# Loading q and k of the first four head pairs in 1 KB pieces, with strided transposes, a shorter warm-up and a divided last store

## The chip, the cores and the metric

The kernel runs on one core of one Trainium2 chip. What counts is the device time of one execution in microseconds: 769.0 us before, the median of three runs (768.95 to 770.54). Engines are named as the profile names them: PE (TensorE; PEld is its weight load), DVE (VectorE), ACT (ScalarE), POOL (GpSimd), SP (SyncE). A letter q behind an engine's name is its queue of DMA issues.

## The reference, cut to what matters

```
q, k, v: (4, 8, 576, 64) f32
scores = q @ k^T / sqrt(64), blocks of 64; block i sees block j where i >= j
attn = softmax(scores);  a = attn @ v
x = a as (2304, 512)                      # 4 batches x 576 rows, 8 heads x 64
h = x @ w_in (512 x 1024);  solu = h * softmax(h);  x = LayerNorm(solu) * g_ln @ w_out
h = x @ w_in2 (512 x 2048); x = (h * tanh(softplus(h))) @ w_out2      # output f32 (2304, 512)
```

## The kernel before, in words

The 32 heads are worked off in 16 pairs, by `pair(p, xt)`; two heads of 64 fill the 128 rows of PE. For each pair q, k and v are loaded in their natural layout, position by position, into the tiles `qraw`, `kraw` and `vraw` (two buffers each). `turn` (L680) lays q or k on its side: five fp32 transposes with `ident`, each of a tile of 128 positions by 2 x 64 columns, into a slot of two PSUM banks; 9 blocks of 64 positions are used, so the fifth tile is half empty (k's upper half is zeroed once; q is shifted by 64 rows and its first half tile zeroed once). ACT copies the result into the high part in fp32r (`act_hi`, L329: `kh`, `qh`), DVE takes the remainder as the low part (`dve_lo`, L335: `kl`; L693: `ql`). The scores are three products of these parts, 64 rows of PE per head (L714), for the first ten pairs with a small product that adds the mask (L722), whose operands are two 64-column pieces `low` of the first `qh` and `ql` buffers. Head 1's keys stand in the opposite order of blocks, so that the triangles of two heads fill one rectangle.

Then come the maximum on DVE (L750, L778), the exponential on ACT (L734), the division on POOL (L792), transposes of the weights (L809), and the product with v (L830, L837). The results go into the first MoE (L895 to L958; SoLU and LayerNorm) and that into the second (L1159, L1251, L1283), whose last piece is `moe2_end` (adds at L1317 and L1325, store at L1339). Weights are loaded and split all along (L449 to L511).

At the start `warm_up` (L1429) gives PE 20 transposes of `ident` before any data are there. `keep_on` (L702) puts 14 more such transposes at two places: ahead of pair 1's last score products (L763, p == 1), and in pair 6.

All of this is first recorded as operations of a `Plan` with engine, cost, priority (the table `PRIO`), what they read and write, and their PSUM slots; `Plan.order` (L146) is a list scheduler that puts them in order for every engine, and they are then emitted in that order. Loads are issued by SP (pair 0's q by ACT). A head of q or k takes one or two DMAs whose pieces are the 256 bytes of one position's 64 numbers:

```
out=r(), in_=rows[r0:r0 + QT * P, :].rearrange("(j p) d -> p j d", p=P)
```

`load` (L629) does this for q and for head 0 of k, `load_k` (L645) for head 1 of k with its blocks reversed, in two DMAs.

Of the kernel before, what the change touches and what calls it, by code (L numbers as in the profile page):

```python
# [260 lines left out]
def c_dma(kb):  # L261
    return max(0.53, kb / 260.0)
# [10 lines left out]
def c_act(n, sbuf=False, acc=False, ptr=False):  # L273
    return 0.05 + n / 1170.0 + 0.04 * sbuf + 0.18 * acc + 0.09 * ptr
# [11 lines left out]
def kernel(  # L286
# [17 lines left out]
    P = 128  # L304
# [23 lines left out]
    def act_hi(dst, src, mul=1.0):  # L328
        nc.scalar.activation(out=dst, in_=src, func=AF.Copy, scale=mul)  # L329
# [18 lines left out]
    def ps2(s):  # L348
        return banks[s.at // 2]
# [212 lines left out]
    HP = H // 2  # L562
    NRAW = 2
    EARLY = 2
    WARM = 20
    qraw = Rot(at, "qraw", NRAW, (P, QT, 2, D), F32)
    kraw = Rot(at, "kraw", NRAW, (P, QT, 2, D), F32)
    vraw = Rot(at, "vraw", NRAW, (P, QT, 2, D), F32)
    nc.vector.memset(qraw.tiles[0][0:64, 0, 0, :], 0.0)
    for i in range(NRAW):  # L570
        nc.vector.memset(kraw.tiles[i][64:128, QT - 1, 1, :], 0.0)
    kh_r = Rot(at, "kh", 2, (P, S), F32R)
# [4 lines left out]
    pt_r = [Rot(at, f"pt{t}_", NPT[t], (P, 2 * EXT[t]), F32) for t in range(QT)]  # L577
    ptw_r = Rot(at, "ptw", NPTW, (P, 2, 512), F32)
    PEMASK = 10
    low = (qh_r.tiles[0][:, 0:64], ql_r.tiles[0][:, 0:64])  # L580
    for i, (x, val) in enumerate(zip(low, (1.0, NEG))):
        raw = ptw_r.tiles[0][:, i, 0:64]
        nc.vector.memset(raw, 0.0)
# [32 lines left out]
    def R1(t):  # L616
        return P if t else 64

    def pair(p, xt):
        b, h2 = divmod(p, HP)  # L620

        def pri(tag, i):
            base, step = PRIO[tag + ("_a" if p < 2 else "" if p < 8 else "_b")]
            return base + step * i
# [20 lines left out]
        def load_k():  # L645
            blocks = k[b, 2 * h2 + 1].rearrange("(j p) d -> p j d", p=64)
            nc.sync.dma_start(out=kr.t[0:64, :, 1, :], in_=blocks[:, 8::-2, :])
            nc.sync.dma_start(out=kr.t[64:128, 0:4, 1, :], in_=blocks[:, 7::-2, :])

        m, go = load(lambda: kr.t[:, :, 0, :], k, n0 * S, False, nc.sync)  # L650
        add(SP, 0.92, go, w=[kr.key(0)], prio=pri("load_k", p))
        add(SP, 1.06, load_k, w=[kr.key(1)], prio=pri("load_k", p))
        for tag, r, src, off, pad in (("load_q", qr, q, -64, False),):
            for x in range(2):

                m, go = load(lambda r=r, x=x: r.t[:, :, x, :], src, (n0 + x) * S + off, pad, nc.sync if p else nc.scalar)
                if p:
                    add(SP, max(m * 0.53, 0.92), go, w=[r.key(x)], prio=pri(tag, p))
                else:
                    add(ACT, 0.5 * m, go, w=[r.key(x)], prio=-2000 + x, lat=2.8)  # L660
        for x in range(2):
            rows = v[b, 2 * h2 + x]

# [13 lines left out]
        def flat(s, n):  # L677
            return ps2(s).rearrange("p a c -> p (a c)")[:, 0:n]

        def turn(r, s):  # L680
            for j in range(QT):
                nc.tensor.transpose(ps2(s)[:, j // 4, (j % 4) * P:(j % 4 + 1) * P],  # L682
                                    r.t[:, j].rearrange("p a d -> p (a d)"), ident)

        sk_, sq_ = Slot(2), Slot(2)
        kk_, kq_ = ("tk", p), ("tq", p)
# [2 lines left out]
        add(DVE, c_dve(S), lambda: dve_lo(kl.t, flat(sk_, S), kh.t), r=[kk_, kh.key()], w=[kl.key()], rel=[sk_],  # L689
            prio=pri("te", p))  # L690
        add(PE, 0.54, lambda: turn(qr, sq_), r=[qr.key(0), qr.key(1)], w=[kq_, qh.key(), ql.key()], acq=[sq_], prio=pri("tr", p))
        add(ACT, c_act(QT * P), lambda: act_hi(qh.t[:, 64:], flat(sq_, QT * P)[:, 64:], scale), r=[kq_], w=[qh.key()], prio=pri("te", p))
        add(DVE, c_dve(QT * P), lambda: nc.vector.scalar_tensor_tensor(  # L693
            out=ql.t[:, 64:], in0=flat(sq_, QT * P)[:, 64:], scalar=scale, in1=qh.t[:, 64:].bitcast(F32), op0=ALU.mult, op1=ALU.subtract),
            r=[kq_, qh.key()], w=[ql.key()], rel=[sq_], prio=pri("te", p))

        on_pe = p < PEMASK
# [4 lines left out]
        def keep_on(dst, n):  # L702
            for _ in range(n):
                nc.tensor.transpose(dst[:, 0:P], ident, ident)

        def mm(items):

            for i, (a, m) in enumerate(((qh, kh), (ql, kh), (qh, kl))):
                for x, t, c0, c1, dst in items:
                    if p == 6 and t == 4 and x == 1 and c0 == i == 0:  # L710
                        keep_on(ps2(s4[0])[:, 1, :], 14)
                    hs = slice(x * D, (x + 1) * D)
                    o = (S - EXT[t]) * x
                    nc.tensor.matmul(out=dst[:R1(t)], lhsT=a.t[hs, (t + 1) * P - R1(t):(t + 1) * P], rhs=m.t[hs, o + c0:o + c1],  # L714
                                     start=(i == 0), stop=(i == 2))
                if i:
                    continue
                for x, t, c0, c1, dst in items if on_pe else ():
                    hs = slice(x * D, (x + 1) * D)
                    a0 = 0 if x else EXT[t] - 64  # L720
                    if t and c0 <= a0 < c1:
                        nc.tensor.matmul(out=dst[0:64, a0 - c0:a0 - c0 + 64], lhsT=low[0][hs], rhs=low[1][hs],  # L722
                                         start=False, stop=False, skip_group_check=True)
# [34 lines left out]
        for ts in (((3, 0), (0, 448)), ((1, 0), (2, 192))):  # L758
            s = Slot(2)
            sk = ("s", p, ts[0][0])  # L760

            def go(s=s, ts=ts):
                if p == 1 and ts[0][0] == 3:  # L763
                    keep_on(ps2(s)[:, 0, :], 14)
                for t, o in ts:
                    mm([(x, t, 0, EXT[t], ps2(s)[:, x, o:o + EXT[t]]) for x in range(2)])

            add(PE, 0.85, go, mode=1, r=qk,
                w=[sk] + [pts[t].key(x) for t, _ in ts for x in range(2)], acq=[s], prio=pri("sc", p))
# [529 lines left out]
    def moe2_end(cnt, g, i, acc):  # L1299
# [36 lines left out]
        to(o1, 2, 1, 1, 0, [acc[2]])  # L1336
        to(o2, 3, 0, 0, 2, [acc[3]])
        for ob, y in tiles:
            add(SP, c_dma(410), lambda ob=ob, y=y: nc.sync.dma_start(out=out[y * P:(y + 1) * P, :], in_=ob.t),  # L1339
                r=[ob.key(0), ob.key(1)] + alias(ob), w=[("out", y)], prio=pri("store", 0))  # L1340

# [198 lines left out]
```

## Time and profile before

| | |
|---|---|
| median of three runs | 769.0 us |
| profiled execution | 769.02 us |
| its span in the profile | 767.2 us |
| PE busy | 754.6 us, 98% |
| DVE, ACT, POOL busy | 566.5, 443.9, 250.1 us |
| share of PE in the chain that ended last | 89% |
| DMA packets, mean rate | 108840, 154 GB/s |
| packets under 512 bytes | 66016 |

The span is what the profiler saw from the first to the last instruction or transfer; the execution's time has 1.8 us around it. In the tables below a time of one instruction is that of its record. Records of PE overlap, as the end of a matmul is modelled, so the step from the start of one to the start of the next tells what one costs, and its record is longer. "x5" joins five neighbours of one kind, and the time beside it goes from the first's start to the last's end. In square brackets stands how long the engine was idle before, and what released it.

### The profile page before, as it was taken

The numbers are of one execution on the slowest core, as the hardware profiler recorded it, in microseconds if no ns is written. First come the engines' busy times: TensorE is split into PE (matmuls) and PEld (weight loads), VectorE is DVE, ScalarE is ACT, GpSimd is POOL, SyncE is SP. The second block draws the span as 40 slices with busy tenths as digits, with TensorE's granted clock in tenths as the row PEclk, the third lists the DMA queues.
The fourth block names the chain that finished last, engine by engine and source line by source line (L and its number), as shares of the span: only waits on it lengthen the run. The fifth ranks groups of instructions, "written<-read, shape, count | busy, mean of one in ns | idle before, by whom it ended". The sixth has DMA issues, their size and how long they took to land.

```text
span 767.2 us, 14951 instructions
## 1 busy us (share of the span) xinstructions
PE 754.6 (98%) x5604; PEld 688.5 (90%) x5604; DVE 566.5 (74%) x1177; ACT 443.9 (58%) x938; POOL 250.1 (33%) x299
## 2 busy tenths in 40 slices
PE   8899999999999999999999999999999999999997
PEld 7788888788888899999998989989988999999997
DVE  6989889999898998876435797562243588569995
ACT  5998897685657555443427554454454664354560
POOL 2687877784574324563130242110000000000000
PEclk9999999999999999999999999999999999999999
DMA  8764653235344364432375566772276571282203
GB/s 190 185 150 98 163 122 108 85 84 174 110 124 149 107 187 130 158 134 79 115 241 195 199 232 224 284 284 77 96 261 205 183 291 56 97 300 76 92 1 111
DMA packets 108840, 118.14 MB, mean 154 GB/s; under 512 B 66016, under 2 KB 77792, under 8 KB 108768
## 3 DMA queue, kind: packets, MB, share of 16 engines
q1 hardware_dynamic: 107504, 116.88, 48.1%
q8 instruction: 44, 0.72, 0.4%
q10 hardware_dynamic: 1264, 0.31, 0.2%
q14 instruction: 28, 0.23, 0.1%
HBM read 76.27 MB, written 40.89 MB: 153 GB/s over the span
## 4 chain that ended last, share of the span: by engine, by line
PE 89%; DVE 6%; ACT 1%; DMA 1%; POOL 1%; issue 1%; SPq 0%; DVEq 0%; ACTq 0%
PE ps L1159 23%; PE ps L895 13%; PE ps L1283 13%; PE ps L958 12%; PE ps L1251 11%; PE ps L714 5%; PE ps L809 4%; PE ps L830 4%; PE ps L942 2%; DVE nmx L778 1%; PE ps L837 1%; PE ps L682 1%; POOL pt L792 1%; ACT pt L734 1%; DVE kl L335 1%
## 5 line engine op out<-in xcount | busy, mean ns | idle before, releaser
L1159 PE MATMUL ps<-wk,w2ih 128*128 128x384 f32 x576 | 147.0, 336 | 1.1 <-ACT xt L1167 1.1
L1159 PEld LDWEIGHTS ps<-wk,w2ih 128*128 128x128 f32 x576 | 102.4, 188 | 2.8 <-ACT xt L1167 1.3
L895 PE MATMUL ps<-wk 128*128 128x512 f32 x432 | 104.6, 396 | 0.0
L792 POOL TENSOR_SCALAR pt<-pt,sm 128x192 f32<-128x192 f32 (+4 forms) x160 | 91.5, 591 | 32.7 <-DVE sm L728 15.7
L1159 PE MATMUL ps<-wk,w2il 128*128 128x384 f32 x288 | 96.8, 336 | 0.0
L895 PEld LDWEIGHTS ps<-wk 128*128 128x128 f32 x432 | 79.4, 188 | 17.1 <-issue 1.1
L734 ACT ACTIVATE pt<-ps,nmx 128x576 f32<-128x576 f32 (+4 forms) x160 | 81.7, 526 | 20.4 <-DVE nmx L778 11.2
L511 POOL TENSOR_TENSOR wem<-wem 128x512 f32<-128x512 f32 x40 | 56.2, 1407 | 83.1 <-DVE wem L508 67.0
L958 PE MATMUL ps<-lth,woh 128*128 128x256 f32 x288 | 81.6, 283 | 0.0
L958 PE MATMUL ps<-lth,wol 128*128 128x256 f32 x288 | 80.9, 281 | 0.0
L958 PE MATMUL ps<-ltl,woh 128*128 128x256 f32 x288 | 80.8, 280 | 0.0
L1283 PE MATMUL ps<-w2oh,cl 128*128 128x512 f32 x144 | 56.1, 390 | 0.0
L958 PEld LDWEIGHTS ps<-lth,wol 128*128 128x128 f32 x288 | 55.1, 191 | 0.1
L1251 PE MATMUL ps<-w2oh,cl 128*128 128x256 f32 x196 | 55.1, 281 | 0.0
L958 PEld LDWEIGHTS ps<-lth,woh 128*128 128x128 f32 x288 | 54.0, 188 | 0.9 <-issue 0.5
L958 PEld LDWEIGHTS ps<-ltl,woh 128*128 128x128 f32 x288 | 54.1, 188 | 0.3
L1159 PEld LDWEIGHTS ps<-wk,w2il 128*128 128x128 f32 x288 | 54.1, 188 | 0.0
L809 PE MATMUL ps<-ident,pt 128*128 128x128 f32 (+1 forms) x400 | 51.0, 274 | 1.5 <-DVE kl L335 0.6
L809 PEld LDWEIGHTS ps<-ident,pt 128*128 128x128 f32 (+1 forms) x400 | 44.6, 141 | 7.5 <-issue 3.3
L778 DVE TENSOR_REDUCE nmx<-ps 128x2 f32<-128x896 f32 (+1 forms) x64 | 40.9, 682 | 6.1 <-PE ps L714 4.3
L506 ACT ACTIVATE wem<-wem,edges 128x512 int32<-128x512 int32 x40 | 29.0, 728 | 19.8 <-DVE wem L452 19.6
L1171 DVE TENSOR_TENSOR xt<-ps,xt 128x384 f32<-128x384 f32 x26 | 14.4, 553 | 33.0 <-PE ps L1159 16.5
(181 smaller groups left out, 1964.5 us busy)
## 6 DMA issues: line engine op xcount, KB each, us to landing
blk_d<-wk SPq DMA_DIRECT2D x36, 384.0 KB, 2.9
wk<-blk_d SPq DMA_DIRECT2D x36, 384.0 KB, 5.4
wraw<-in_moe_w_in_dram SPq DMA_DIRECT2D x24, 512.0 KB, 4.4
park_d<-wem SPq DMA_DIRECT2D x20, 448.0 KB, 2.6
wraw<-in_moe_w_out_dram SPq DMA_DIRECT2D x16, 512.0 KB, 3.8
wem<-park_d SPq DMA_DIRECT2D x18, 448.0 KB, 4.1
qraw<-in_q_dram SPq DMA_DIRECT2D x30, 160.0 KB, 3.2
x_d<-xo SPq DMA_DIRECT2D x18, 256.0 KB, 2.4
```

The lines of the kernel that those rows point to most:

```text
L511: add(POOL, c_tt(wd), lambda: nc.gpsimd.tensor_tensor(out=mf(), in0=mf(), in1=ex().bitcast(F32), op=ALU.mult), r=[ek], w=[mk], **pt)
L714: nc.tensor.matmul(out=dst[:R1(t)], lhsT=a.t[hs, (t + 1) * P - R1(t):(t + 1) * P], rhs=m.t[hs, o + c0:o + c1], start=(i == 0), stop=(i == 2))
L734: add(ACT, c_act(EXT[t], acc=True), lambda: nc.scalar.activation(out=pp.t[0:R1(t), x * EXT[t]:(x + 1) * EXT[t]] if t < 4 else pp.t[:, x * ...
L778: add(DVE, 2 * c_dve(512), lambda s=s, ts=ts: [nc.vector.tensor_reduce(out=nmx.t[0:R1(t), :, t], in_=ps2(s)[0:R1(t), :, o:o + EXT[t]], axi ...
L792: nc.gpsimd.tensor_scalar(pp, pp, sm.t[0:R1(t), x, t:t + 1], 1.0, op0=ALU.mult, op1=ALU.mult)
L809: nc.tensor.transpose(ps2(s)[:, a, o + P - n:o + P], pts[t].t[0:n, c * P:(c + 1) * P], ident[0:n, 0:n])
L830: nc.tensor.matmul(out=ps(os_[r])[x * D:(x + 1) * D, o:o + n_], lhsT=vr.t[:, j, x, :], rhs=packs[pi].t[:, a, c0:c0 + n_], start=(i in (0, ...
L895: nc.tensor.matmul(out=ps2(hp)[:, hf, :], lhsT=x.t[:, kk, :], rhs=w[:, kk, hf * 512:(hf + 1) * 512], start=bool(first), stop=bool(last))
L958: nc.tensor.matmul(out=ps(s)[:, (c % 2) * 256:(c % 2) * 256 + 256], lhsT=w[:, kk, cs], rhs=x.t[:, kk, :], start=(kk == 0 and i == 0), stop ...
L1159: nc.tensor.matmul(out=ps(s)[:, 0:HT], lhsT=sl_i[j, w][:, c, a, :], rhs=x.t[:, mv], start=(start and c == 0 and i == 0), stop=(c == 1 and ...
L1251: nc.tensor.matmul(out=ps(acc[bi])[:, h * 256:(h + 1) * 256], lhsT=x.t[:, a], rhs=sl_o[j, w][:, b], start=(first and h == 0 and y == 0), s ...
L1283: nc.tensor.matmul(out=ps(acc[t]), lhsT=x.t[:, 2 * t + f], rhs=plain(j, w, f), start=(first and f == 0 and y == 0), stop=(last and f == 1 ...
```

## The change

For pairs 0 to 3 (`WIDE`) q and k are loaded in pieces of four positions, 1 KB each: partition p gets positions 4p to 4p+3 of the head (of q from position 64 on, of k's head 0 from 0 on, of head 1 from 64 on), and the 64 positions that remain of each head come as a small DMA for both heads. The number of DMAs that SP issues for a pair stays (k three in two steps of the plan, q two); pair 0's q has two instead of three on ACT. `turn` follows for these pairs with 9 transposes instead of 5: for head 1 four of 128 columns, of which the upper 64 rows of the result are used and the lower ones written over; for head 0 four of 64 columns; and one of 64 rows for both heads' ends. The first eight write every fourth column of the PSUM bank (head 1 of k with the blocks reversed).

For pairs 4 to 15 the pieces stay at 256 bytes, and the fifth transpose is now one of 64 rows. All pairs have q's last 64 positions in the last place, so the memset of `qraw` is gone, the tiles are read by `q_at`, and the mask's `low` pieces move to columns 576 to 640. The warm-up has 14 transposes. Pair 1's 14 idle ones are left out, pair 6's stay. The last output tile's store is two DMAs of 256 columns each. The order of everything else, and the PSUM banks, are those of before on every engine.

```diff
-    WARM = 20
+    WARM = 14
+    WIDE = 4
...
-    nc.vector.memset(qraw.tiles[0][0:64, 0, 0, :], 0.0)
...
-    low = (qh_r.tiles[0][:, 0:64], ql_r.tiles[0][:, 0:64])
+    low = (qh_r.tiles[0][:, S:], ql_r.tiles[0][:, S:])
...
+    def q_at(t):
+        return slice((t - 1) * P, t * P) if t else slice(512, 576)
...
+        wide = p < WIDE
+
+        def most(r):
+            return r.t.rearrange("p j x d -> p (j x d)")[:, 0:8 * D]
+
+        def q_wide(x):
+            eng = nc.sync if p else nc.scalar
+            heads = q[b, 2 * h2:2 * h2 + 2]
+            if x:
+                eng.dma_start(out=qr.t[0:64, 4], in_=heads[:, 0:64].rearrange("x p d -> p x d"))
+            else:
+                eng.dma_start(out=most(qr).rearrange("p (x c) -> p x c", x=2),
+                              in_=heads[:, 64:].rearrange("x (p j) d -> p x (j d)", j=4))
+
+        def k_wide(x):
+            head = k[b, 2 * h2 + x]
+            rows = head[64:] if x else head[0:512]
+            nc.sync.dma_start(out=most(kr)[:, 4 * D * x:4 * D * (x + 1)], in_=rows.rearrange("(p j) d -> p (j d)", j=4))
+            if x:
+                ends = k.rearrange("b h s d -> (b h s) d")[n0 * S + 512:n0 * S + 640]
+                nc.sync.dma_start(out=kr.t[0:64, 4], in_=ends.rearrange("(x p) d -> p x d", x=2))
...
         def turn(r, s):
-            for j in range(QT):
-                nc.tensor.transpose(ps2(s)[:, j // 4, (j % 4) * P:(j % 4 + 1) * P],
-                                    r.t[:, j].rearrange("p a d -> p (a d)"), ident)
+            if wide:
+                to = ps2(s)[:, 0, :].rearrange("p (a c j) -> p j a c", a=8, j=4)
+                for x in (1, 0):
+                    for j in range(4):
+                        a = 4 * D * x + j * D
+                        o = to[0:D + D * x, j]
+                        nc.tensor.transpose(o[:, ::-1] if x and r is kr else o, most(r)[:, a - D * x:a + D], ident)
+                y, o = r.t[0:64, 4], 0
+            else:
+                a = 0 if r is kr else 1
+                for j in range(4):
+                    nc.tensor.transpose(ps2(s)[:, 0, j * P:(j + 1) * P], r.t[:, j + a].rearrange("p x d -> p (x d)"), ident)
+                o = 64 * a
+                y = r.t[o:o + 64, 0 if a else 4]
+            nc.tensor.transpose(ps2(s)[:, 1, 0:64], y.rearrange("p x d -> p (x d)"), ident[o:o + 64, o:o + 64])
...
-                if p == 1 and ts[0][0] == 3:
-                    keep_on(ps2(s)[:, 0, :], 14)
...
+            if last_group(cnt) and i == 2 and ob is o2:
+                for h in (1, 0):
+                    add(SP, c_dma(205), lambda ob=ob, y=y, h=h: nc.sync.dma_start(
+                        out=out[y * P:(y + 1) * P, h * 256:(h + 1) * 256], in_=half_of(ob, h)),
```

The places in the order that the prediction speaks of follow. In a row stand the line, the operation, the PSUM tile that is written (`ps_63` to `ps_66` are the four two-bank tiles), what it reads, and the size; `qraw_96`, `qraw_97`, `kraw_98` and `kraw_99` are the two buffers of each. Rows of the changed kernel have its own line numbers: L712 and L717 are the transposes of a wide and of a narrow turn, L720 the last one of 64 rows, L751 the scores, L844 the weights' transposes.

PE at the start of the program, before:

```order
L1429 MATMUL ps_63<-ident 128x128 x20
L682 MATMUL ps_63<-ident,qraw_96 128x128 x5
L682 MATMUL ps_64<-ident,kraw_98 128x128 x5
L682 MATMUL ps_65<-ident,kraw_99 128x128 x5
L714 MATMUL ps_66<-kh_105,qh_109 128x288
```

and changed:

```order
L1470 MATMUL ps_63<-ident 128x128 x14
L712 MATMUL ps_63<-ident,qraw_96 128x128 x4
L712 MATMUL ps_63<-ident,qraw_96 64x128 x4
L720 MATMUL ps_63<-ident,qraw_96 128x64
L712 MATMUL ps_64<-ident,kraw_98 128x8x16 x4
L712 MATMUL ps_64<-ident,kraw_98 64x128 x4
L720 MATMUL ps_64<-ident,kraw_98 128x64
L712 MATMUL ps_65<-ident,kraw_99 128x8x16 x4
L712 MATMUL ps_65<-ident,kraw_99 64x128 x4
L720 MATMUL ps_65<-ident,kraw_99 128x64
L751 MATMUL ps_66<-kh_104,qh_108 128x288
```

Six transposes of the warm-up are gone, and the turns of pair 0's q and k and of pair 1's k have 27 instead of 15 ahead of the first scores.

PE ahead of pair 1's scores, before:

```order
L714 MATMUL ps_65<-kl_107,qh_109 128x320 x2
L682 MATMUL ps_66<-ident,qraw_96 128x128 x5
L682 MATMUL ps_63<-ident,qraw_97 128x128 x5
L704 MATMUL ps_63<-ident 128x128 x14
L714 MATMUL ps_63<-kh_106,qh_110 128x448 x2
```

and changed:

```order
L751 MATMUL ps_65<-kl_106,qh_108 128x320 x2
L712 MATMUL ps_66<-ident,qraw_96 128x128 x4
L712 MATMUL ps_66<-ident,qraw_96 64x128 x4
L720 MATMUL ps_66<-ident,qraw_96 128x64
L712 MATMUL ps_63<-ident,qraw_97 128x128 x4
L712 MATMUL ps_63<-ident,qraw_97 64x128 x4
L720 MATMUL ps_63<-ident,qraw_97 128x64
L751 MATMUL ps_63<-kh_105,qh_109 128x448 x2
```

The idle transposes between q's turns and the scores are gone, and the two turns have 18 transposes instead of 10.

PE at the first turns of pair 4, the first narrow ones, before:

```order
L682 MATMUL ps_64<-ident,kraw_98 128x128 x5
L682 MATMUL ps_66<-ident,qraw_96 128x128 x5
L809 MATMUL ps_65<-ident,pt_1_116 128x128
L809 MATMUL ps_65<-ident,pt_1_118 128x128
L809 MATMUL ps_65<-ident,pt_1_120 128x128
```

and changed:

```order
L717 MATMUL ps_64<-ident,kraw_98 128x128 x4
L720 MATMUL ps_64<-ident,kraw_98 128x64
L717 MATMUL ps_66<-ident,qraw_96 128x128 x4
L720 MATMUL ps_66<-ident,qraw_96 128x64
L844 MATMUL ps_65<-ident,pt_1_115 128x128
L844 MATMUL ps_65<-ident,pt_1_117 128x128
L844 MATMUL ps_65<-ident,pt_1_119 128x128
```

Each turn's fifth transpose has become one of 64 columns; what follows stands where it stood.

## Rows read from the trace of the kernel before

**Rows 1.** The page: span, busy time of each engine, chain that ended last by engine.

```profile
span 767.2 us, 14951 instructions
PE 754.6 (98%) x5604; PEld 688.5 (90%) x5604; DVE 566.5 (74%) x1177; ACT 443.9 (58%) x938; POOL 250.1 (33%) x299
PE 89%; DVE 6%; ACT 1%; DMA 1%; POOL 1%; issue 1%; SPq 0%; DVEq 0%; ACTq 0%
```

**Rows 2.** Stretches: length, busy PE PEld DVE ACT POOL, clock, DMA, GB/s.

```profile
25.00:110.00 85.00, 83.63 (x988) 70.86 (x987) 75.24 (x130) 75.43 (x211) 68.80 (x94) 1.00 0.58 141
110.00:195.00 85.00, 84.32 (x710) 70.56 (x709) 79.06 (x163) 62.48 (x151) 58.10 (x77) 1.00 0.41 116
```

**Rows 3.** Timeline and chain, first 9 us: start, duration, what.

```profile
1.34 4.33 PE L1429 MATMUL ps<-ident 128*128 128x128 f32 x20 [1.34 <-POOL ident masks.py:199]
3.95 3.81 DMA kraw<-in_k_dram
5.84 0.74 PE L682 MATMUL ps<-ident,qraw 128*128 128x128 f32 x5 [0.17 <-DMA qraw<-in_q_dram]
7.80 0.77 PE L682 MATMUL ps<-ident,kraw 128*128 128x128 f32 x5 [0.68 <-DMA kraw<-in_k_dram]
8.50 0.53 PE L714 MATMUL ps<-kh,qh 64*128 64x288 f32 x4
```

**Rows 4.** Timeline of PE at two places near 238 and 240 us.

```profile
237.94 0.47 PE L809 MATMUL ps<-ident,pt 128*128 128x128 f32 x2
238.15 0.13 PEld L809 LDWEIGHTS ps<-ident,pt 64*128 64x128 f32 x1 [0.17 <-issue]
238.35 0.44 PE L942 MATMUL ps<-ident,e 128*128 128x128 f32 x2
...
239.93 0.38 PE L942 MATMUL ps<-ident,e 128*128 128x128 f32 x2
240.25 0.44 PE L830 MATMUL ps<-ptw,vraw 128*64 128x256 f32 x2
```

**Rows 5.** Timeline, 11 to 25 us.

```profile
11.63 1.49 PE L682 MATMUL ps<-ident,qraw 128*128 128x128 f32 x10
12.50 1.31 ACT L329 ACTIVATE qh<-ps 128x576 fp32r<-128x576 f32 x2 [0.20 <-PE ps L682]
14.65 1.75 PE L704 MATMUL ps<-ident 128*128 128x128 f32 x14 [1.53 <-DVE ql L693]
17.51 1.28 DVE L778 TENSOR_REDUCE nmx<-ps 128x2 f32<-128x896 f32 x2 [0.76 <-PE ps L714]
18.89 0.63 ACT L734 ACTIVATE pt<-ps,nmx 128x448 f32<-128x448 f32 x1 [0.86 <-DVE sm L728]
21.01 0.77 PE L682 MATMUL ps<-ident,qraw 128*128 128x128 f32 x5 [1.58 <-ACT pt L734]
21.73 0.76 PE L682 MATMUL ps<-ident,kraw 128*128 128x128 f32 x5
22.39 1.06 PE L809 MATMUL ps<-ident,pt 128*128 128x128 f32 x8
23.62 0.77 PE L682 MATMUL ps<-ident,kraw 128*128 128x128 f32 x5 [0.17 <-DVE ql L693]
```

**Rows 6.** Turns from 25 us on: group by form, and two places of the chain.

```profile
L682 PE MATMUL ps<-ident,kraw 128*128 128x128 f32 x60 | 9.1, 282 | 0.2 <-ACT pt L734 0.2
...
108.89 1.24 PE ps L682 x10
...
157.71 1.09 PE ps L682 x10
```

**Rows 7.** The end: timeline, and DMA issues (KB each, us to landing).

```profile
763.40 0.41 DVE L1317 TENSOR_TENSOR xo<-ps,xo 128x256 f32<-128x256 f32 x1
763.93 0.38 SPq L1339 DMA_DIRECT2D out_dram<-xo  x1
...
out_dram<-xo SPq DMA_DIRECT2D x9, 256.0 KB, 2.0
```

More of the change, by code (lines that the diff above doesn't have):

```diff
@@ L648, in load_k @@
             nc.sync.dma_start(out=kr.t[64:128, 0:4, 1, :], in_=blocks[:, 7::-2, :])
-        m, go = load(lambda: kr.t[:, :, 0, :], k, n0 * S, False, nc.sync)
[L651 to L660, printed above, removed]
+        wide = p < WIDE
@@ new lines, in pair @@
+        add(SP, 0.92, (lambda: k_wide(0)) if wide else go, w=[kr.key(0)], prio=pri("load_k", p))
+        add(SP, 1.06, (lambda: k_wide(1)) if wide else load_k, w=[kr.key(1)], prio=pri("load_k", p))
+        for x in range(2):
+            m, go = load(lambda x=x: qr.t[:, :, x, :], q, (n0 + x) * S - 64, False, nc.sync)
+            if wide:
+                go = lambda x=x: q_wide(x)
+            if p:
+                add(SP, max(m * 0.53, 0.92), go, w=[qr.key(x)], prio=pri("load_q", p))
+            else:
+                add(ACT, 0.5 * m, go, w=[qr.key(x)], prio=-2000 + x, lat=2.8)
@@ L680, in turn @@
         def turn(r, s):
-            for j in range(QT):
-                nc.tensor.transpose(ps2(s)[:, j // 4, (j % 4) * P:(j % 4 + 1) * P],
-                                    r.t[:, j].rearrange("p a d -> p (a d)"), ident)
+            if wide:
+                to = ps2(s)[:, 0, :].rearrange("p (a c j) -> p j a c", a=8, j=4)
[5 more added lines that the diff above has]
+                y, o = r.t[0:64, 4], 0
+            else:
+                a = 0 if r is kr else 1
[4 more added lines that the diff above has]
+            nc.tensor.transpose(ps2(s)[:, 1, 0:64], y.rearrange("p x d -> p (x d)"), ident[o:o + 64, o:o + 64])
         sk_, sq_ = Slot(2), Slot(2)
@@ L691, in pair @@
         add(PE, 0.54, lambda: turn(qr, sq_), r=[qr.key(0), qr.key(1)], w=[kq_, qh.key(), ql.key()], acq=[sq_], prio=pri("tr", p))
-        add(ACT, c_act(QT * P), lambda: act_hi(qh.t[:, 64:], flat(sq_, QT * P)[:, 64:], scale), r=[kq_], w=[qh.key()], prio=pri("te", p))
+        add(ACT, c_act(QT * P), lambda: act_hi(qh.t[:, 0:S], flat(sq_, S), scale), r=[kq_], w=[qh.key()], prio=pri("te", p))
         add(DVE, c_dve(QT * P), lambda: nc.vector.scalar_tensor_tensor(
-            out=ql.t[:, 64:], in0=flat(sq_, QT * P)[:, 64:], scalar=scale, in1=qh.t[:, 64:].bitcast(F32), op0=ALU.mult, op1=ALU.subtract),
+            out=ql.t[:, 0:S], in0=flat(sq_, S), scalar=scale, in1=qh.t[:, 0:S].bitcast(F32), op0=ALU.mult, op1=ALU.subtract),
             r=[kq_, qh.key()], w=[ql.key()], rel=[sq_], prio=pri("te", p))
@@ L713, in mm @@
                     o = (S - EXT[t]) * x
-                    nc.tensor.matmul(out=dst[:R1(t)], lhsT=a.t[hs, (t + 1) * P - R1(t):(t + 1) * P], rhs=m.t[hs, o + c0:o + c1],
+                    nc.tensor.matmul(out=dst[:R1(t)], lhsT=a.t[hs, q_at(t)], rhs=m.t[hs, o + c0:o + c1],
                                      start=(i == 0), stop=(i == 2))
@@ L1338, in moe2_end @@
         for ob, y in tiles:
+            if last_group(cnt) and i == 2 and ob is o2:
+                for h in (1, 0):
+                    add(SP, c_dma(205), lambda ob=ob, y=y, h=h: nc.sync.dma_start(
+                        out=out[y * P:(y + 1) * P, h * 256:(h + 1) * 256], in_=half_of(ob, h)),
+                        r=[ob.key(h)] + alias(ob), w=[("out", y, h)], prio=pri("store", 0))
+                continue
             add(SP, c_dma(410), lambda ob=ob, y=y: nc.sync.dma_start(out=out[y * P:(y + 1) * P, :], in_=ob.t),
```

## The prediction

> **What bounds the kernel now.** I read first the page's share of busy time and the chain that ended last [rows 1]: TensorE (PE) is busy for 754.6 us of a span of 767.2, and 89% of the chain lies on PE, 6% on VectorE (DVE), 1% each on ScalarE (ACT) and on DMA. So PE time that is added on the chain is added to the span, nearly one for one, and a faster transfer is worth something only where PE waits for it. Next I read PE's busy time by stretch [rows 2]: of the 170 us from 25 to 195, in which the pairs 4 to 15 are worked off, PE stands idle for 170.00 - 83.63 - 84.32 = 2.05 us. There is hardly a hole in which added PE work could vanish. Then the start [rows 3], the prices of PE's steps [rows 4], the stretch from 11 to 25 us [rows 5], the places of the turns on the chain [rows 6] and the end [rows 7].
>
> The profiled execution took 769.02 us, which is the median of the three runs (769.0), so the sum below can be put on either.
>
> **The price of a step.** A transpose in a run of its like costs what 14 idle ones show: 1.75 us, less some 0.33 that the last one is still recorded after its start, is 13 steps of 0.109 us [rows 5]. A change of the tile's shape costs more. In [rows 4] two transposes begin at 237.94, the first of 128 rows and the second of 64 (the weight load of the second is the row at 238.15), and the next one of 128 rows begins at 238.35: 0.41 us for two steps, 0.20 into the 64-row one and 0.20 out of it. From 239.93 to 240.25 there are two 128-row transposes and then a matmul with a 128x64 stationary: 0.32 - 0.109 = 0.21 for the step to half the columns. So I take 0.20 for every change of shape.
> A turn of five was 5 x 0.109 = 0.545 us. **Narrow turn** (pairs 4 to 15): three steps of 0.109, one into the 64-row transpose, one out of it, 0.73: +0.18 each. **Wide turn** (pairs 0 to 3): 3 x 0.109, 0.20 to half columns, 3 x 0.109, 0.20 to the 64 rows, 0.20 out, 1.25: +0.71 each.
> The Trainium skill ("TensorE: Matmul & The Clock Gate", section "Back-to-back issue gap") gives 64 columns about 60 cycles against 134 for 128, by which the 64-row transpose would be cheaper than the one that it replaces. The rows above have 0.20 there, so the measurement decides; what the rule would make of the time is the first rival.
>
> **A, the start (0.0).** Before, 20 transposes run from 1.34 to 5.67 at 0.213 a step, twice 0.109, so at the lower of the two clock levels (1.2 against 2.4 GHz); q's five begin at 5.84 and end 0.74 us later, 4 x 0.109 and 0.30 for the last one's record, so they have the step of the upper level, and the rise came ahead of them; I put it at 5.4 us. The third turn waits for the k of pair 1, issued at 3.95 and landed at 7.76, and the scores begin at 8.50 [rows 3]. After, 14 transposes end at 1.34 + 14 x 0.213 = 4.3 us. If the 1 KB pieces have landed by then, three wide turns take 3.78 us, and half of the time up to 5.4 is lost to the lower level: 4.4 + 0.5 + 3.8 = 8.7, less the last step out, which disappears since the scores have 64 rows as well: 8.5. What the transfers give, the 12 added transposes take. Bounds: no added price, -0.7; transfers no faster than before, third turn from 7.80, scores at 9.1, +0.6. Both ends stay. The moved `low` columns, the dropped memset and one DMA issue less on ACT cost nothing: nobody waits for them there, since PE's first wait is for q [rows 3].
>
> **B, 11.6 to 18.9 us (+0.45).** Two turns for q begin at 11.63; ACT's two copies (12.50, 1.31 us together) follow, then DVE's low halves, and the idle transposes, which had to wait for these (1.53 us), begin at 14.65 [rows 5]. Two wide turns finish 1.42 us later, the second copy and low half move by about 1.25, and the scores, with 1.75 us of idle transposes gone, begin at 16.4 (14.65 + 1.75) + 1.25 - 1.75 = 15.9. That gain isn't kept: DVE, 1.25 late, has only the 0.76 us that it waited ahead of pair 1's maximum (17.51) to give back, so the maximum and ACT's exponentials behind it (18.89, with 0.86 of wait) come 0.45 to 0.5 later. Bounds: -0.76 (both waits closed by earlier scores) and +1.25.
>
> **C, 21.0 to 24.4 us (+1.75).** Three wide turns stand here, at 21.01, 21.73 and 23.62: 3 x 0.71 = 2.13. Eight transposes of 0.109 from 22.39 end at 23.26, the third turn began at 23.62: 0.36 us of slack, so 2.13 - 0.36 = 1.77 [rows 5]. Bounds: 0.7 (the third turn alone) and 2.1.
>
> **D, pairs 4 to 15 (+1.5).** 60 transposes of k [rows 6] are 12 turns, and there are 12 of q: 24 x 0.18 = 4.4 us of PE. On the chain stand 6 of the 24, of which [rows 6] has the first two and the last two: 6 x 0.18 = 1.1. The others lie where the chain goes through DVE or ACT, and there PE can take up at most its visible idle time of 2.05 us [rows 2], which leaves 2.4. Between 1.1 and 2.4 I take 1.5, nearer to the chain's count, because waits shorter than a matmul's modelled tail don't show as idle. Bounds 0 (as if a 64-row step cost no more) and 4.4.
>
> **E, the end (-0.3).** The last add ends at 763.81, the store of xo is issued at 763.93 and the span ends at 767.2 [rows 7]. Half of that store now goes ahead of the other tile's, and half as many bytes are left behind the last add. A 256 KB store takes 2.0 us from issue to landing [rows 7]; most of that can't be bytes, as the transfer has the tile before it to follow. Bounds -0.6 and 0.
>
> **Sum:** 0.0 + 0.45 + 1.75 + 1.5 - 0.3 = +3.4; 769.0 + 3.4 = **772.4 us**.
>
> **The rivals.**
> *Switches are free* (not slower). If a narrow instruction costs its columns and the load of its weights is pulled ahead, a wide turn is 8 x 0.109 + 0.055 = 0.93 (+0.38), and the last of a narrow one saves 0.055. Start -0.7, B 0 (DVE's 0.76 covers it), C 3 x 0.38 - 0.36 = +0.8, D 24 x -0.055 = -1.3, of which as in D a third counts, -0.5, end -0.3: -0.7, 768.3. It decides below about 0.13 us a switch. Against it stand the steps of [rows 4]; for it, that those are seen at a few places and with other neighbours. Chance 0.13.
> *The transfers set everything up to 24 us* (faster). If PE's extra transposes are as good as free and data are there by 6 us, the scores start 1.5 earlier (the third turn from 6.3 instead of 7.80), pair 1's follow without the idle transposes (-0.76), C is 0, D and the end give -0.8 as above: 766.0. For it: the waits for DMA and DVE in [rows 3, 5]; against: 98% busy PE. Chance 0.09.
> *The clock rises later.* With a shorter warm-up, and gaps if data are late, the rise at 5.4 may come behind the turns: at most 3.4 us more (the 3.8 us of turns at half speed), 775.8. Against it: before, nothing but transposes had run when the step fell from 0.213 to 0.109 [rows 3]. Or PE, idle longer ahead of pair 1's scores without the 14 transposes, falls back to the lower level there. Together 0.06. The Trainium skill ("TensorE: Matmul & The Clock Gate", section "Part 4: PE-mode transpose") says that transposes don't count as busy for the clock; the trace disagrees, by the step that halves after 20 of them.
> *Writes with a stride cost.* 64 wide transposes write every fourth column. No row of before has such a write; at 0.03 us each, 1.9 us in all, 774.3. Chance 0.07.
> *The change doesn't do what it says*: 1 KB pieces land no earlier, A is +0.6, 773.0. Chance 0.05.
>
> **How the numbers follow.** Forecast 0.60, mostly within 770.6 and 774.2. A measurement of this kernel tells apart about 0.2%, 1.5 us. Faster by more: the second rival and a third of the first, 0.13. Within: the rest of the first and the low tail of the forecast (D and C near their lower ends), 0.18. Slower: 0.69. The range 767.6 to 775.0 leaves out the transfers' rival (0.09), most of the clock's (0.06), and the ends of the stride's and the first one's (0.05).
>
> **What would show it.** PE's rows of the turns: 24 with a fifth transpose that begins 0.20 after the fourth, and its follower 0.20 after that; 8 that take 1.25 us from first to next. The scores of pair 0 at 8.5, of pair 1 at 15.9, DVE's first maximum of pair 1 at 18.0, PE at +2.2 where the third wide turn ends, +3.7 at 195 us and from there on constant. If the steps at the 64-row transposes are 0.06 to 0.11, the sum falls and the first rival holds; if scores start below 7.5, the second; if the turns at the start have steps of 0.2 throughout, the clock's.

## The result, and the profile of the changed kernel

The changed kernel takes 773.02 us (median of six runs, 772.47 to 776.23), before 769.05 in the same comparison: a ratio of 1.0052, with an interval of 1.0034 to 1.0070, or +4.0 us. Forecast were +3.4 us, 772.4, slower with a chance of 0.69.

The profiled execution is the longest of the six, 776.23 us, with a span of 774.4, and it is 3.2 us above the median for reasons that can be read, a late rise of the clock and a fall. The lines of the page that answer to [rows 1]:

```profile
span 774.4 us, 14974 instructions
PE 765.8 (99%) x5616; PEld 696.1 (90%) x5616; DVE 566.8 (73%) x1176; ACT 445.5 (58%) x938; POOL 250.0 (32%) x299
PE 95%; DVE 3%; ACT 1%; issue 0%; POOL 0%; DVEq 0%; POOLq 0%; ACTq 0%
```

PE has 11.2 us more than before [rows 1] and its weight loads 7.6; DVE, ACT and POOL are within 1.6 us of what they had. Of the chain that ended last 95% lie on PE, before 89%. By stretch (columns as in [rows 2]; the number behind POOL's is the granted clock):

```profile
6.00:25.00 19.00, 16.79 (x140) 13.66 (x139) 13.53 (x32) 12.94 (x39) 6.66 (x12) 0.81 0.60 164
25.00:110.00 85.00, 84.97 (x939) 72.15 (x939) 73.09 (x125) 73.61 (x204) 64.02 (x89) 0.98 0.58 143
110.00:195.00 85.00, 84.62 (x722) 68.67 (x720) 76.60 (x156) 64.21 (x158) 58.13 (x74) 1.00 0.38 103
...
14.00:16.00 2.00, 1.06 (x9) 0.72 (x7) 0.89 (x2) 1.49 (x3) 0.00 (x0) 1.00 0.01 3
16.00:18.00 2.00, 1.41 (x18) 1.26 (x20) 1.83 (x7) 2.00 (x11) 0.47 (x1) 0.92 0.70 199
18.00:20.00 2.00, 2.00 (x20) 1.80 (x20) 2.00 (x7) 2.00 (x8) 2.00 (x4) 0.50 0.87 211
...
26.00:28.00 2.00, 2.00 (x11) 1.71 (x10) 0.74 (x1) 1.42 (x6) 1.05 (x3) 0.52 0.61 139
28.00:30.00 2.00, 2.00 (x19) 1.74 (x18) 1.32 (x3) 1.68 (x6) 0.00 (x0) 1.00 0.57 130
```

The hole of 2.05 us from 25 to 195 is down to 0.41. And the clock is at the lower level, 0.50, from about 17.7 to 27.9 us: it falls behind the place where the 14 idle transposes stood (PE busy for 1.06 of 2 us from 14 to 16). Of the three wide turns that follow, the first two (22.08 and 24.28) run at half speed, the third doesn't:

```profile
24.28 1.97 PE L712 MATMUL ps<-ident,kraw 128*128 128x128 f32 x8
...
28.09 1.04 PE L712 MATMUL ps<-ident,kraw 128*128 128x128 f32 x8
```

This run has a mean clock of 0.993, the other five have 0.997 to 0.999, so less of it. The mean leaves the start out: the profiles give the first 6 us as 1.00, though the warm-up's steps there are 0.213 us, those of the lower level [rows 3]. A late rise lowers no mean.

PE's timeline shows the prices (start, duration, what):

```profile
1.34 3.25 PE L1470 MATMUL ps<-ident 128*128 128x128 f32 x14 [1.34 <-POOL ident masks.py:199]
4.39 1.91 PE L712 MATMUL ps<-ident,qraw 128*128 128x128 f32 x8
6.52 1.52 PE L712 MATMUL ps<-ident,kraw 128*128 128x128 f32 x8
9.21 0.58 PE L751 MATMUL ps<-kh,qh 64*128 64x288 f32 x4
...
12.53 1.09 PE L712 MATMUL ps<-ident,qraw 128*128 128x128 f32 x8 [0.19 <-ACT pt L771]
13.56 0.27 PE L720 MATMUL ps<-ident,qraw 64*128 64x64 f32 x1
13.76 1.09 PE L712 MATMUL ps<-ident,qraw 128*128 128x128 f32 x8
...
16.59 0.47 PE L751 MATMUL ps<-kh,qh 64*128 64x448 f32 x2 [1.53 <-DVE ql L730]
18.61 1.26 DVE L813 TENSOR_REDUCE nmx<-ps 128x2 f32<-128x896 f32 x2
...
37.40 0.66 PE L717 MATMUL ps<-ident,kraw 128*128 128x128 f32 x4
37.98 0.27 PE L720 MATMUL ps<-ident,kraw 64*128 64x64 f32 x1
38.19 0.66 PE L717 MATMUL ps<-ident,qraw 128*128 128x128 f32 x4
38.77 0.27 PE L720 MATMUL ps<-ident,qraw 64*128 64x64 f32 x1
38.98 0.66 PE L844 MATMUL ps<-ident,pt 128*128 128x128 f32 x4
```

A wide turn takes 13.76 - 12.53 = 1.23 us (forecast 1.25), a narrow one 38.19 - 37.40 = 0.79 (forecast 0.73). The starts of the single transposes tell why. A narrow turn's steps are 164, 109, 109, 203 and, out of the 64-row one, 203 ns: the step out and the step in are the forecast's 0.20, but the first transpose after a change of rows also takes 164 instead of 109 (in the rows: three steps of a narrow turn are 0.66 less the 0.27 of one record, 0.39, where 3 x 0.109 is 0.33). A wide turn's are 164, 109 x 6, 203 and 204: there is nothing at the place where the stationary operand (the one that is loaded ahead, here the data) goes from 128 to 64 columns, and the writes to every fourth column cost nothing. The 1.23 us came out right because two errors in it cancel.

The way from one kernel to the other can be followed at two places, the first 24 products with v that are on the chain, and the run of 213 matmuls near its end. Of before:

```profile
28.53 2.31 PE ps L830 x24
736.81 25.10 PE ps L1251 x213
```

and of the changed kernel:

```profile
33.25 2.31 PE ps L865 x24
744.36 25.10 PE ps L1286 x213
```

Up to the first place +4.72 us, from there to the second another 7.55 - 4.72 = 2.83, and from the second to the end -0.3 (774.4 - 744.36 = 30.04 against 767.2 - 736.81 = 30.39, with spans rounded to 0.1).

### The profile page after: what moved, and what is told of

It is laid out like the page before. It is cut to its first block, busy times and chain, and to the rows that moved or that the text cites. A ratio compares the mean times of both kernels' runs of the same rounds, so it can differ in the third digit from the quotient of the medians.

```text
span 774.4 us, 14974 instructions
## 1 busy us (share of the span) xinstructions
PE 765.8 (99%) x5616; PEld 696.1 (90%) x5616; DVE 566.8 (73%) x1176; ACT 445.5 (58%) x938; POOL 250.0 (32%) x299
## 4 chain that ended last, share of the span: by engine, by line
PE 95%; DVE 3%; ACT 1%; issue 0%; POOL 0%; DVEq 0%; POOLq 0%; ACTq 0%
PE ps L1194 23%; PE ps L930 13%; PE ps L1318 13%; PE ps L993 12%; PE ps L1286 11%; PE ps L844 6%; PE ps L751 5%; PE ps L865 4%; PE ps L977 2%; PE ps L717 2%; PE ps L712 1%; PE ps L872 1%; PE ps L720 1%; DVE nmx L813 1%; ACT pt L771 1%; PE ps L1470 0%
## 5 line engine op out<-in xcount | busy, mean ns | idle before, releaser
L844 PE MATMUL ps<-ident,pt 128*128 128x128 f32 (+1 forms) x400 | 50.6, 277 | 0.0
L844 PEld LDWEIGHTS ps<-ident,pt 128*128 128x128 f32 (+1 forms) x400 | 44.8, 142 | 4.7 <-issue 2.5
```

What stands on the lines that cost most here:

```text
L844: nc.tensor.transpose(ps2(s)[:, a, o + P - n:o + P], pts[t].t[0:n, c * P:(c + 1) * P], ident[0:n, 0:n])
```

## The experiments

Five rounds each. Most expectations set two theories against each other: by that of the steps the whole loss is PE's dearer turns, by that of the clock a part of it is the fall to the lower level. "At full clock" means the runs whose mean clock is 0.999 or 1.000. The kernel before, run beside each experiment, has 768.4 to 769.4 there in all but three of its runs (771.4, 771.6, and one of 1907 that is in no ratio), and 769.2 to 773.0 in those with 0.997 or 0.998. A mean of 0.998 stands for some 1.5 us of lost clock in 770, so the longest of these probably have another cause too; no trace shows it.

**1. The idle transposes back in the changed kernel** (e1_idle_back).

```diff
             def go(s=s, ts=ts):
+                if p == 1 and ts[0][0] == 3:
+                    keep_on(ps2(s)[:, 0, :], 14)
```

> The changed kernel with pair 1's 14 idle transposes put back, nothing else. Theory of the steps (the whole loss is PE's dearer steps in the turns): the idle transposes cost 0 to 0.5 us, 773.0 to 773.5, and the turns at 22 us stay as long as in the changed kernel in a run at full clock. Theory of the clock (without them PE falls to the lower clock level at about 18 us, as the profiled run of the changed kernel shows from 17.8 to 28): granted clock 1.00 in every stretch behind 6 us, and 1.5 to 2.5 us faster than the changed kernel, 770.5 to 771.5.

Measured: 775.17 us, ratio 1.0072 (1.0055 to 1.0088). The runs fall into two groups: 773.06 and 773.53 with a clock of 1.000, and 774.8 to 775.7 with 0.998. The profiled one is of the first group and has a clock of 1.00 in every stretch. Both theories miss. The idle transposes do hold the clock there in this run, but four of six have a lower mean; where the clock fell in these no trace shows, and they are 2.2 us longer, more than 0.998 accounts for. Even at full clock the kernel is slower than the changed one at its best (772.47 with 0.999). So by these few runs leaving them out is worth 0.6 to 1.1 us at full clock, where the theory of the steps had 0 to 0.5. From the profile, which has no low clock behind the start, the terms can be read apart:

```profile
4.39 1.41 PE L712 MATMUL ps<-ident,qraw 128*128 128x128 f32 x8
8.18 0.59 PE L751 MATMUL ps<-kh,qh 64*128 64x288 f32 x4
11.51 1.09 PE L712 MATMUL ps<-ident,qraw 128*128 128x128 f32 x8 [0.18 <-ACT pt L771]
...
21.92 1.09 PE L712 MATMUL ps<-ident,qraw 128*128 128x128 f32 x8 [1.57 <-ACT pt L771]
26.48 0.76 PE L846 MATMUL ps<-ident,pt 128*128 128x128 f32 x5
...
30.46 2.31 PE ps L867 x24
741.66 25.10 PE ps L1288 x213
```

At the first place it is 1.93 us behind before, at the second 4.85: the start, B and C together 1.9 with the idle transposes in, and pairs 4 to 15 2.9. C alone is +1.13: from the first of its three turns to what follows the third 26.48 - 21.92 = 4.56 us, before 24.44 - 21.01 = 3.43 ([rows 5], and the chain of before:)

```profile
24.44 2.14 PE ps L809 x17
```

**2. The idle transposes out of the kernel before** (e2_idle_out): the two lines above removed from `go`.

> The kernel before, only without pair 1's 14 idle transposes. Theory of the steps: pair 1's scores come up to 1.75 us earlier, DVE's wait of 0.76 us is given back at most: 768.2 to 769.0. Theory of the clock: the granted clock falls below 1 somewhere from 15 to 28 us, and the time rises by 1.5 to 3 us, 770.5 to 772.

Measured: 769.10 us, 0.9996 (0.9987 to 1.0005): no difference, and again neither theory: the clock does fall, but at another price. The profiled run (769.97) has

```profile
11.00:17.00 6.00, 4.42 (x48) 3.39 (x44) 5.75 (x15) 5.80 (x21) 1.41 (x2) 0.94 0.84 242
17.00:23.00 6.00, 5.20 (x32) 4.59 (x31) 5.32 (x16) 5.46 (x17) 5.21 (x11) 0.50 0.63 142
```

so six to seven us at half clock, and it costs what the missing transposes give: the first products with v begin at 28.48, before at 28.53. (The 0.9 us that this run took more than before arise at full clock: from the 24 products that begin at 147.71 in both, the next 24 on the chain begin at 221.82, before at 220.93.) All twelve runs have 0.995 to 0.999; the one with 0.999 took 768.10.

**3. and 4. Narrow turns alone**, in two orders. In e3_rows64 the 64-row transposes stand last in k's turn and first in q's; in n2_rows64_last both stand last, as in the changed kernel; the edit below is n2's, e3 leaves the order of the loop as it was.

```diff
-            for j in range(QT):
-                nc.tensor.transpose(ps2(s)[:, j // 4, (j % 4) * P:(j % 4 + 1) * P],
-                                    r.t[:, j].rearrange("p a d -> p (a d)"), ident)
+            for j in range(QT) if p < 4 or r is kr else (1, 2, 3, 4, 0):
+                rows = slice(0, P) if p < 4 or j != (4 if r is kr else 0) else slice(0, 64) if r is kr else slice(64, P)
+                nc.tensor.transpose(ps2(s)[:, j // 4, (j % 4) * P + rows.start:(j % 4) * P + rows.stop],
+                                    r.t[rows, j].rearrange("p a d -> p (a d)"), ident[rows, rows])
```

> The kernel before, only with the half-empty tile of pairs 4 to 15 (k's last, q's first) turned by a 64-row transpose; loads, start, idle transposes and store as before. Forecast for this term: +1.5 us, 770.5 (bounds 0 and 4.4). By the profile of the changed kernel, where the offset grows from 4.7 us at 30 to 7.5 at 206: +2.8, 771.8. Rival (switches free): 768.5. The step after the 64-row transpose is 0.20, and the one after that 0.165 instead of 0.109.

> The kernel before with narrow turns in pairs 4 to 15 in the changed kernel's own order: the 64-row transpose stands last in k's turn and in q's (in the run with 64-row transposes in before's order they were neighbours, 4 ns apart, so that a pair paid for one change of rows, not two). Forecast for this term: +1.5, 770.5. Theory of the steps as measured since: a turn costs 164+109+109+203+203 ns = 0.79 us against 0.545, 24 x 0.24 = 5.9 us of PE, of which about half shows, +2.8: 771.5 to 772.2. If the run at 770.5 was all there is: 770.5.

Measured: 770.49 us (1.0018, 1.0010 to 1.0026) and 771.79 us (1.0033, 1.0022 to 1.0044). The first looks like the forecast's 1.5, but it is another case: where q's turn follows k's, the two 64-row transposes are neighbours and use different rows of PE, the second begins 3 or 4 ns after the first, and two turns pay for one change of rows. In the rows of e3 k's last record begins with q's first, at 32.71 + 0.86 - 0.27 = 33.30:

```profile
32.71 0.86 PE L683 MATMUL ps<-ident,kraw 128*128 128x128 f32 x5
33.30 0.86 PE L683 MATMUL ps<-ident,qraw 64*128 64x64 f32 x5
```

The second run, n2, is the term D itself: +2.83 us. Its profiled run has the prices of the changed kernel, 33.60 - 32.81 = 0.79 for a turn, and between the two places on the chain 711.12 us, the changed kernel 711.11, before 708.28:

```profile
32.81 0.86 PE L683 MATMUL ps<-ident,kraw 128*128 128x128 f32 x5
33.60 0.86 PE L683 MATMUL ps<-ident,qraw 128*128 128x128 f32 x5
34.39 0.44 PE L810 MATMUL ps<-ident,pt 128*128 128x128 f32 x2
...
28.66 2.31 PE ps L831 x24
739.78 25.10 PE ps L1252 x213
```

24 turns x 0.244 = 5.9 us of PE, counted by steps (with the dearer first step of what follows a turn), of which 48% are seen in the time.

**5. The divided store alone** (s1_store): before, with the loop over `h` of the change's last hunk.

> The kernel before, only with the last output tile's store in two halves. Forecast: -0.3 us, so 768.7; bounds 768.4 and 769.1. The offset of the changed kernel shrinks by 0.35 us between its last matmul and its end.

Measured: 768.77 against 768.96 us, 0.9995 (0.9985 to 1.0005). The gain of 0.2 is too small to be told from none by the times; in the traces it does show: the way from the last run of matmuls to the end is 30.0 to 30.2 us in every kernel with the divided store, 30.4 in every one without, so 0.2 to 0.35 us shorter (0.23 here).

**6. No change of rows in any turn** (f1_rows128): the last transpose takes all 128 rows, and q's 64 rows in the upper half are brought to the front by exchanging the halves of the identity.

```diff
-            nc.tensor.transpose(ps2(s)[:, 1, 0:64], y.rearrange("p x d -> p (x d)"), ident[o:o + 64, o:o + 64])
+            turned = ident.rearrange("p (h c) -> p h c", h=2)
+            nc.tensor.transpose(ps2(s)[:, 1, 0:P].rearrange("p (h c) -> p h c", h=2),
+                                y.rearrange("p x d -> p (x d)"), turned[:, ::-1] if o else turned)
```

(`y` is then the whole tile; the unused rows of the last tile are zeroed at the start.)

> The changed kernel, but the last transpose of every turn takes all 128 rows (for q with the halves of the identity exchanged), so that no turn changes the tile's rows; the unused rows of the last tile are zeroed once. Theory of the steps: narrow turns are back at 0.545, wide ones at 1.04: the term of pairs 4 to 15 (2.8 us) and about 0.5 to 1 of the wide ones go: 769.2 to 770.0. Theory of the clock: the lower level stays (granted clock below 1 between 16 and 28 us), so the time stays above that of before by 1.5 to 2.5: 770.0 to 771.5 with the steps gone, 772 to 773 if they cost nothing.

Measured: 768.31 us, 0.9995 (0.9981 to 1.0008). Seven runs with a clock of 0.999 or 1.000 take 767.90 to 768.35, five with 0.995 take 770.48 to 770.97. So both theories hold, each in its place: without the changes of rows the changed kernel is 4.3 us faster at full clock (its one run with 0.999, 772.47, against about 768.1), 2.8 of them in pairs 4 to 15 as in n2, which leaves some 1.5 for the wide turns; and the runs with a lower clock are 2.7 us longer. The profiled run is one of the five. Its clock rises late, at 7.3 us, as well as falling at 17.6, so the 2.7 may hold both; between the two places on the chain it takes 708.24 us, before 708.28, so in pairs 4 to 15 no loss is left:

```profile
17.00:23.00 6.00, 5.05 (x39) 4.10 (x38) 5.64 (x17) 5.46 (x20) 5.20 (x11) 0.55 0.67 165
23.00:30.00 7.00, 7.00 (x63) 6.62 (x62) 4.82 (x10) 5.43 (x13) 3.22 (x6) 0.90 0.63 142
...
30.85 2.31 PE ps L867 x24
739.09 25.10 PE ps L1288 x213
```

**7. The same with the idle transposes back** (f2_rows128_idle), and **8. with these and a warm-up of 20** (f3_rows128_idle_warm20).

> The changed kernel with every last transpose over 128 rows and pair 1's idle transposes back, warm-up 14. Against 768.1 (clock 1.00) and 770.8 (clock 0.995) of the same without idle transposes: theory of the clock: one group only, with a clock of 0.998 or more, at 768.1 + 1.0 = 769.1 (the idle transposes' own price, by the changed kernel with and without them at full clock). If the idle transposes don't guard the clock: two groups again, 769.1 and 771 or more.

> The changed kernel with every turn's last transpose over all 128 rows, pair 1's idle transposes put back and the warm-up at 20: what is left of the change are the 1 KB pieces, 9 transposes in a wide turn and the divided store. Theory of the clock: the granted clock is 1.00 in all or nearly all runs, so no second group 2.5 us higher as without the idle transposes. Time: wide turns +0.44 each, of which some +1 in all on the chain, the store -0.35: 769.2 to 770.2. If the transfers' lead were worth more than the four added transposes per turn: 768.0 to 768.6.

Measured: 769.39 us (0.9997, 0.9986 to 1.0009) and 770.29 us (1.0012, 0.9996 to 1.0029). In f2 all twelve runs have a clock of 0.999 or 1.000 and lie between 768.7 and 770.2: the idle transposes do guard the clock there, for about 1.1 us, by which the median is above that of f1; the mean of all runs is nearly the same (769.45 against 769.21). In f3 ten of twelve runs are in one group, 769.3 to 770.7; the other two took 772.51, with a clock of 1.000, and 773.54. From f2 to f3 six more transposes at the start cost 0.9 at the median, though the two intervals overlap.

**9. The warm-up at 20 in the changed kernel** (e4_warm20).

> The changed kernel with the warm-up back at 20 transposes; everything else as changed. Forecast (term A is zero: what the data's lead gives, the added transposes take): the turns start at 5.7 at the upper level, 27 transposes of 3.7 us, first scores at 9.3, +0.3 to +0.7: 773.2 to 773.8. Theory of the late rise (the shorter warm-up lets the clock rise at 7.2 instead of 5.4, as the profiled run has it, first scores at 9.2): the rise comes before 6.0 again, first scores at 9.3 all the same, 772.8 to 773.3, and the share of runs with a later fall of the clock does not change.

Measured: 774.31 us, 1.0059 (1.0044 to 1.0074), 1.3 above the changed kernel and above both forecasts. In the profiled run the clock rises at 4.3 us, while the warm-up is still running, and the turns ahead of the first scores have the upper level throughout; it falls later here too, from 21.4 to 24.8:

```profile
1.35 3.84 PE L1470 MATMUL ps<-ident 128*128 128x128 f32 x20 [1.35 <-POOL ident masks.py:199]
5.02 1.04 PE L712 MATMUL ps<-ident,qraw 128*128 128x128 f32 x8
8.45 0.59 PE L751 MATMUL ps<-kh,qh 64*128 64x288 f32 x4
...
17.00:23.00 6.00, 3.93 (x38) 3.12 (x38) 5.74 (x17) 5.56 (x21) 5.23 (x10) 0.87 0.66 163
```

The rise, where the step of the transposes halves, comes at another time in every execution: in the profiled runs of this study between 4.1 and 7.4 us, and with the very same start at 5.1 (e1) and 7.4 (the changed kernel). In e1 the first scores begin at 8.18, in the changed kernel at 9.21. So the shorter warm-up does not bring a late rise every time. But it isn't cleared of it: of the seven profiles with a warm-up of 14 four rise at 7.2 to 7.4 and three at 4.1 to 5.4, the seven with 20 all at 4.3 to 6.0. By the times the shorter warm-up is worth about 1 us all the same (1.3 here, 0.9 from f2 to f3).

**10. Pair 1's q ahead of pair 2's** (g1_swap): f1 with three pairs of operations exchanged in the finished order.

```diff
     order = plan.order()
+    for n in range(3):
+        first, second = (plan.ops[plan.q_of[i] + n] for i in (1, 2))
+        order.remove(second)
+        order.insert(order.index(first) + 1, second)
```

> The changed kernel with every last transpose over 128 rows, and q's turn, copy and low half of pair 1 put ahead of those of pair 2 on PE, ACT and DVE, so that PE's wait ahead of pair 1's scores gets shorter by a turn or a low half. If that wait is what lets the clock fall, the group of runs near 770.8 with a clock of 0.995 disappears or gets rare, and the median is 767.5 to 768.2; if the clock's fall depends on when the whole stretch comes and not on this wait, the two groups (768.1 and 770.8) stay. DVE has the same work ahead of pair 1's maximum, so the runs at full clock are the same or up to 0.5 faster.

Measured: 770.14 us, 1.0011 (1.0000 to 1.0022), a miss: 769.3 to 770.0 at full clock, 770.3 to 771.2 with 0.995 or 0.996, six runs each. The first turn begins later, 12.68 instead of 12.00 in f1, as the PSUM slot of pair 1's q is freed by a later exponential on ACT. PE's wait ahead of pair 1's scores is down to 0.55 us, in f1 1.53, and the groups are still two, so that wait isn't all that decides on the fall.

**11. and 12. Only pairs 0 and 1 wide** (h1_wide2: f1 with `WIDE = 2`; h2_wide2_idle: the same with the idle transposes).

> The changed kernel with every last transpose over 128 rows and only pairs 0 and 1 in 1 KB pieces (pairs 2 and 3 in turns of five): the three turns at 21 to 24 us and one of the two at 12 us are back at 0.55 to 0.60 us. Theory of the steps: 4 x 0.44 = 1.8 us less PE, about half on the chain: 767.2 to 767.7 at full clock, below both kernels; with the clock's fall 2 to 2.7 more. If the turns of pairs 2 and 3 were hidden: 768.1.

> The same with pair 1's 14 idle transposes back. Theory of the clock: one group, clock 0.998 or more, 1.0 above the other's full-clock group: 768.2 to 768.7. If leaving them out gains nothing at full clock: 767.2 to 767.7 here as well.

Measured: h1 768.52 us, 0.9985 (0.9974 to 0.9996), 767.2 to 767.6 at full clock (four runs), 768.4 to 769.7 with 0.995 to 0.998. h2 768.65 us, 0.9989 (0.9980 to 0.9999), 768.1 to 769.5, eleven of twelve runs at 1.000. At the median both lie 0.4 to 0.5 us below the kernel before and 4.4 to 4.5 below the changed one. The former is within the 0.2% that the prediction gives a measurement of this kernel, though the intervals just exclude no change. In the profiled run of h1 (clock 1.00, and at 4.1 us the earliest rise of all profiles) the gain is made at the start:

```profile
27.00 2.31 PE ps L867 x24
735.51 25.10 PE ps L1288 x213
```

1.53 us ahead of before at the first place, 1.30 at the second.

## Why the prediction was right, and where its steps were not

The sign, the cause (PE's dearer turns) and the sum were right, the terms less so. That the sum came within 0.6 us is partly luck: D was 1.3 too low, and the start, B and C together 0.7 too high.

- **The prices of the steps.** 0.20 into and out of a 64-row transpose: right, in every narrow turn and in the wide ones at the upper level. 0.20 for half the columns: wrong, among transposes it costs nothing. I had read it from one place where a matmul with a 128x64 stationary follows a 128-row transpose [rows 4]; what is dear there isn't the number of columns of a transpose, and what it is was not tried. What I missed is the first step after a change of rows, 164 instead of 109 ns; a turn of five that follows scores, which use 64 rows, shows it in before too, had I looked at single starts instead of groups. Narrow: +0.24 instead of +0.18; wide: 1.23, forecast 1.25.
- **D** is the step that failed most: +1.5 forecast, +2.83 measured (n2). A third of that gap is the price per turn, the rest the share that shows: I counted the turns on the chain, 1.1, and leaned to that end of 1.1 to 2.4. The other argument, that PE had only 2.05 us of idle time to take work up, was the better one: of 5.9 us added, about half shows. The count itself was one short, as the chain of before has a turn at 32.75 as well, and it was the wrong thing to count. Added work on PE moves the chain: in the changed kernel's trace all 24 narrow turns stand on it, before 7.

```profile
32.75 0.71 PE ps L682 x5
```

- **A, B and C.** Forecast 2.2 together; the median leaves 4.0 - 2.83 + 0.3 = 1.5, in which is what the clock took in those runs. The traces put it thus: up to the first products with v +1.9 at full clock with the idle transposes in (e1), and, as an estimate, about 1 less without them. C was too high: +1.13 in e1 for +1.75, as two of its three turns took 0.72 and 0.66 us before (21.73 - 21.01 and 22.39 - 21.73 in [rows 5]), not 0.545. B was too high as well: I let DVE swallow what the idle transposes give back, but taking them out is worth 1.0 us at full clock in three comparisons (the changed kernel and e1, f1 and f2, h1 and h2: 0.6 to 1.3 us each); at the median the fall of the clock took it back where it was tried alone (e2). A was right as a middle: the first scores began at 8.18 and at 9.21 in two executions with the same start, before at 8.50. Of the marks that were set, pair 0's scores at 8.5, pair 1's at 15.9 and DVE's first maximum of pair 1 at 18.0, the profiled run has 9.21, 16.59 and 18.61, all 0.6 to 0.7 late by the late rise; B's own 0.45 is in the last one. The third wide turn ends 2.04 us later than before in e1 (26.48 against 24.44; the mark was +2.2) and 4.8 later in the changed kernel's profile, and near 195 us that has +7.8 (its last turn begins at 200.04, before at 192.21) where the mark was +3.7; from 221 us on it is constant at 7.5.
- **E**: -0.3 forecast, -0.3 in the traces.
- **The rivals.** *Switches are free*: excluded, by the steps, by n2 and by f1. *Transfers*: the pieces do land early, as q's turn follows the warm-up with no wait at 4.39 and k's has none either, but what their lead is worth by itself was not measured. f3, which keeps the pieces, the nine transposes (now over 128 rows) and the divided store and takes the rest back, is not faster than before (770.29, 1.0012), and h1 with half of the wide turns is 0.6 us faster at full clock than f1 with all. *Writes with a stride*: excluded, 109 ns. *The clock*: it was given 0.06, and both of its halves happen in part of the runs. A late rise is in four of the seven profiles with the shorter warm-up. As to the fall, all six runs of the changed kernel had a mean below 1.000, though so had 37 of the 91 runs of the kernel before, with its idle transposes. Where the runs fall in two groups, those with the lower clock are longer by 1.1 us (h1), 1.4 (g1), 2.2 (e1) and 2.7 (f1); how much of this is the fall and how much a late rise isn't shown. The chance was set too low: the run with both took 776.23, beyond the range.

The Trainium skill ("TensorE: Matmul & The Clock Gate", section "Back-to-back issue gap") gives a matmul over 64 moving columns about 60 cycles against 134 for 128, and so would have made the 64-row transposes, which have 64, cheaper. The trace disagrees: 203 ns for one of them, against 109. The Trainium skill ("TensorEngine Tiling (Array Packing)", section "Key Properties") also says that changing the tiling mode drains the engine. The trace shows a price that agrees with it for rows (203 ns in, 203 out, 164 for the next); for columns it shows none among the wide turn's transposes (109 ns from 128x128 to 128x64).

What stays open: what decides in a run whether the clock falls behind 16 us. f1 and g1 have about the same work there and show both; with the idle transposes back a lower mean was rare (none of twelve in f2, one in h2), but not in e1 (four of six), of which no trace shows where. Open too is whether the shorter warm-up makes a late rise likelier.

## What to carry to other kernels

A transpose with half the rows is dearer than a full one that is half empty: fill the tile with zeros and keep the shape of the stretch (f1), or, second best, put two half ones on different rows side by side (e3). Where PE is busy for 98%, price an edit by all of PE's time that it adds, about half of which showed here, rather than by the instructions of it that lie on the chain of before: the chain moves. Where idle work that keeps the clock up is taken away, look at the mean clock of every run and not at one profile: the median can stay while the runs split in two groups. A mean that leaves out the start doesn't show a late rise; the steps of the first transposes do.

## What the runs showed that was not expected

- The time of the clock's rise differs between executions of the same start by over 2 us (5.1 and 7.4), and with it the first scores by 1.0 us.
- Leaving 14 idle transposes out of a stretch where PE waits gains 1.0 us at full clock and loses it again by a clock at the lower level, for 6.8 us in the profiled run of e2: before with and without them is the same to 0.1% (e2).
- Two 64-row transposes on different halves of PE's rows start 3 to 4 ns apart, and so cost one change of rows between them (e3 against n2: 1.3 us in all).
- Transposes with a stationary operand of 64 columns behind ones of 128 keep the step of 109 ns.
